# One queue order for conversions and splits, and three passes on split weights for groups of 128 rows, in an attention, MoE and MoE kernel

## The chip, the cores and the metric

One core of one Trainium2 chip. The metric is the device time of one execution in microseconds (us), the median of several runs. The engines are PE (TensorE, with its weight load PEld), DVE (VectorE), ACT (ScalarE), POOL (GpSimd) and SP (SyncE, which here issues most DMAs). Each engine takes its instructions in the order of the program and waits on semaphores.

## The reference

Three layers one after the other, in float32:

```python
# attention: 4 batches, 8 heads, 576 positions, 64 wide; window of 128, ALiBi slopes
scores = where(mask, scale * q @ k.T + bias, -1e9)
x = softmax(scores) @ v                      # as [2304, 512]
# first MoE (a dense MLP): w_in 512 x 2048, w_out 2048 x 512, float64 inputs taken as pairs of words
x = softplus(x @ w_in) @ w_out
# second MoE: 8 experts, top 2 of noisy logits; w1 512 x 1024, w2 1024 x 512 each
noisy = x @ w_gate + softplus(x @ w_noise) * noise
out[rows of expert e] += weight * (relu(x[rows] @ w1[e]) @ w2[e])
```

The result must hold to float32-like accuracy, so a product of two numbers is made of three matmuls on a high and a low half (hi·hi, hi·lo, lo·hi) in the type fp32r, or of one matmul on plain float32.

## The kernel before

The tokens go in 9 chunks of 256 (`NCH`), the hidden width of the first MoE in 16 pieces of 128 (`NF`). A job (c, f) is the up step `mm1` and, three jobs later, the down step `mm2` of piece f for chunk c. The first pieces (`NA` = 6) of chunk 0 and chunk 1 are interleaved, then those of each later chunk; attention runs beside them, a piece of it after each step (`side_work`), since chunk c needs its attention rows. The other ten pieces of all chunks follow.

The first MoE's weights come as 32 tiles of 64-bit words. `w_convert` turns one into high and low halves: a load on SP, three ACT steps (L486, L490, L500), three DVE steps of bits (L494 to L496), an add on POOL (L512), and the subtraction that gives the low half on DVE or, for some, on POOL (L504); eight are stored to DRAM and read back. At most five conversions (`NCV`) are under way; 12 may be started before the first job, the others with the jobs.

Attention's step a makes scores (PE L339), adds bias and takes the row minimum (DVE L350), exponentials (ACT L356), reciprocals (DVE L361, L362), and normalises on POOL (L370) or ACT (L368). Step b transposes (PE L201), step c multiplies with v (PE L190) and makes the high and low halves of x (ACT L429, DVE L434).

The softplus of `mm1` takes ACT, DVE and POOL steps (L565 to L574); L568, which reads the PSUM tile, frees it for PE.

The second MoE works on groups of rows of one expert: 18 pairs (256 rows) and 5 small groups (128 rows) that always run, and 2 more under a condition. The first four pairs are built from an early table, the others after the last routing. A group's w1 and w2 come as 4 tiles of 512 KB each. For pairs the order of load is one w1 tile, one w2 tile, and so on; for a small group four w1 tiles, then four w2 tiles (`WJ`). `w2_load` loads a tile as soon as the ring of 24 slots has room; `w2_split` makes its halves, `whi` on ACT (L1141) and `wlo` on DVE (L1139), for at most `NSPLIT` = 5 tiles that are not yet used up; `w2_free` runs when a tile's last matmul has been issued, and calls `pump`, which loads and splits again. Small groups use the unsplit float32 tile, and `skip_singles` passes them over when splitting.

At each step `s1` (up) of an item runs, then the transposes of the next group's rows, `s2` (transposes of a small group's hidden rows) of the item before, and `s3` (down) of the item two before. So a group's last `s3` stands after the first two `s1` of the group that follows. A pair has 8 items, a small group 2.

What sets the order on the engines is the class `Order`, a planner that runs while the program is written. `chain` gives it steps with an engine and an estimated cost; `need` and `spend` move its clock on along PE. Steps are taken from a heap by the time at which they become ready, and their instructions are issued in that order. PE's own instructions are issued directly, in the order of the loops.

Of the kernel before, what the change touches and what calls it, by code (L numbers as in the profile page):

```python
# [9 lines left out]
F32 = mybir.dt.float32  # L10
# [15 lines left out]
class Order:  # L26
# [8 lines left out]
        self.free = {}  # L35
        self.parked = {}

    def chain(self, *steps, after=0.0):

        heapq.heappush(self.heap, (self.now + after, self.count, steps, 0))  # L40
        self.count += 1

    def done(self, key, when):
# [2 lines left out]
            heapq.heappush(self.heap, (max(when, entry[0]),) + entry[1:])  # L46

    def _pop(self):
        entry = when, count, steps, i = heapq.heappop(self.heap)
        eng, cost, fn, key, needs = (tuple(steps[i]) + (None,) * 5)[:5]  # L50
        for n in needs or ():
            if n not in self.fin:
                self.parked.setdefault(n, []).append(entry)
                return
            if self.fin[n] > when:
                heapq.heappush(self.heap, (self.fin[n], count, steps, i))
                return
        if eng is not None:
            when = max(when, self.free.get(eng, 0.0))
        end = when + cost  # L60
        if eng is not None:
            self.free[eng] = end
        if fn is not None:
            fn()
        if key is not None:
            self.done(key, end)
        if i + 1 < len(steps):
            heapq.heappush(self.heap, (end + (0.1 if eng is not None else 0.0), count, steps, i + 1))

    def emitted(self, key):  # L70
        while key not in self.fin:
# [24 lines left out]
def ca(n):  # L96
    return 0.16 + n * 0.00083
# [15 lines left out]
def moe_chain_kernel(ctx, tc, qk, v, w_in, w_out, w_gate, w_noise, noise, w1, w2, out):  # L113
# [362 lines left out]
    def w_convert(i):  # L476
        fc, half = divmod(i, 2)
        d = {}

        def load():  # L480
            raw = d["raw"] = wpool.tile([P, 512, 2], I32, name="raw", tag="w", bufs=NRING)
            SP.dma_start(raw.rearrange("p n z -> p (n z)"), (w_out if half else w_in).bitcast(I32)[fc])

        def first():
            d["a"] = tl(mid, [P, 512], I32, "cva", 4, ("wl", i))
            ACT.activation(f32(d["a"]), f32(d["raw"][:, :, 1]), AF.Abs)  # L486

        def third():
            lo32 = d["raw"][:, :, 0]
            ACT.activation(lo32, lo32.bitcast(U32), AF.Copy, scale=2.0 ** -29)  # L490

        def bits():
            a = d["a"]
            DVE.tensor_scalar(f32(a), f32(a), F64_LO, F64_HI, op0=OP.max, op1=OP.min)  # L494
            DVE.tensor_scalar(a, a, 3, 0x3FFFFFFF, op0=OP.logical_shift_left, op1=OP.bitwise_and)  # L495
            DVE.scalar_tensor_tensor(a, d["raw"][:, :, 1], -0x40000000, a, op0=OP.bitwise_and, op1=OP.bitwise_or)  # L496

        def high():
            W[i] = w_tile()
            ACT.activation(W[i][:, 0], f32(d["a"]), AF.Copy)  # L500

        def low():
            t = W[i]
            (DVE if (i < 2 * NA or LOWV[i % len(LOWV)]) else POOL).tensor_tensor(t[:, 1], f32(d["a"]), f32(t[:, 0]), OP.subtract)  # L504

        def store():
            if i in sidx:
                SP.dma_start(scratch[sidx.index(i)], f32(W.pop(i)).rearrange("p z n -> p (z n)"))
                nfreed[0] += 1
        chain(("SP", 0.06, load), ("DMA", (1 << 19) / 330e3, None), (None, 2.0, None),  # L510
              ("A", ca(512), first), ("A", ca(512), third), ("V", 2.2, bits),
              ("P", cg(512), lambda: POOL.tensor_tensor(d["a"], d["a"], d["raw"][:, :, 0], OP.add), ("wa", i)),  # L512
              ("A", ca(512), high),
              ("V", cv(512), low, ("wl", i)) if (i < 2 * NA or LOWV[i % len(LOWV)]) else ("P", cg(512), low, ("wl", i)),
              (None, 0.0, lambda: mark_now(("w", i), ("wl", i))),
              ("SP", 0.06, store, ("st", i)))

    def mark_now(key, of):
        o_.done(key, o_.fin[of])
# [533 lines left out]
    def g_transpose(g, a):  # L1053
        n, eo, i = groups[g]
        d = GR[g]
        pt = ps_t(("gx", g, a)).rearrange("p (c t) -> p c t", c=KC)
        for kc in range(KC):
            tr(pt[:, kc, :], d["xg"][a][:, kc * P:(kc + 1) * P], ident)
        if n == 1:
            d["xT"] = tl(p2, [P, KC, P], F32, "xs", 2, ("gup", g))  # L1060
            return chain(("A", ca(512), lambda: ACT.activation(d["xT"], pt, AF.Copy), ("gx", g, a)))
        if a == 0:
            d["xT"] = tuple(tl(mid, [P, KC, CT], F32R, x, 2, ("gup", g)) for x in ("xh", "xl"))
        xh, xl = d["xT"]
        sl = slice(a * P, (a + 1) * P)
        chain(("A", ca(512), lambda: ACT.activation(xh[:, :, sl], pt, AF.Copy)),
              ("V", cv(512), lambda: DVE.tensor_sub(xl[:, :, sl], pt, f32(xh[:, :, sl])), ("gx", g, a)))
# [20 lines left out]
    def w2_load():  # L1088
        j = wl[0]
        if j >= NW:  # L1090
            return False
        g, kind, f = WJ[j]
        if g >= sure[0] or ("tab", 2 if groups[g][0] == 1 else int(g >= NEARLY)) not in o_.fin:
            return False
        more = len(extra) < NXTRA
        if not more and (nback[0] < len(sidx) or ring_left() < 1 + 2 * max(1, NSPLIT - nsplit[0])):
            return False
        wl[0] += 1
        n, eo, i = groups[g]
        if g not in REG:  # L1100
            REG[g] = SP.value_load(TB[eo][0:1, 0, i:i + 1], min_val=0, max_val=E - 1)
            g_rows(g)
            if g < 3 or g - 3 in turned:
                g_start(g)
        if more:
            extra.add(j)
            t = p2.tile([P, 1024], F32, name="raw2", tag="raw2", bufs=NXTRA)
        else:
            inring[0] += 1
            t = wpool.tile([P, 1024], F32, name="rawp", tag="w", bufs=NRING)  # L1110
        RAW2[j] = t
        SP.dma_start(t, (w2 if kind else w1)[bass.ds(REG[g], 1), f].rearrange("e p n -> p (e n)"))
        chain(("SP", 0.5, None), ("DMA", (1 << 19) / 280e3, None), (None, 2.5, None, ("r2" if n == 2 else "w2", j)))
        if n == 1 and wsp[0] == j:
            skip_singles()
        return True

    turned = set()
# [2 lines left out]
        n = groups[g][0]  # L1121
        chain(("P", 1.3 * n, lambda: g_gather(g), ("gg", g), (("rows", g),)), (None, 3.0, None, ("gl", g)))

    def skip_singles():
        while wsp[0] < wl[0] and groups[WJ[wsp[0]][0]][0] == 1:
            wsp[0] += 1

    def w2_split():
        skip_singles()
        j = wsp[0]  # L1130
        if j >= wl[0] or not splitting[0] or nsplit[0] >= NSPLIT or nback[0] < len(sidx) or ring_left() < 2:
            return False
        wsp[0] += 1
        nsplit[0] += 1
        t = RAW2[j]
        hi, lo = W2[j] = [wpool.tile([P, 1024], F32R, name=x, tag="w", bufs=NRING) for x in ("whi", "wlo")]

        def low():
            DVE.tensor_sub(lo, t, f32(hi))  # L1139
            w2_drop(j)  # L1140
        chain(("A", ca(1024), lambda: ACT.activation(hi, t, AF.Copy), None, (("r2", j),)),  # L1141
              ("V", cv(1024), low, ("w2", j)))
        return True

    def w2_drop(j):
# [11 lines left out]
                pass  # L1157

    def w2_free(j):
        if W2.pop(j, None) is None:  # L1160
            w2_drop(j)
        else:
            nsplit[0] -= 1
        pump()

    def parts(j, a):
        hl = W2[j]
        if WJ[j][1] == 0:
            return lambda z, kc: hl[z][:, kc * 256 + a * P:kc * 256 + (a + 1) * P]
        return lambda z: hl[z][:, a * 512:(a + 1) * 512]  # L1170
# [4 lines left out]
    def s1(g, f):  # L1175
# [15 lines left out]
        else:  # L1191
            need(("gx", g, 0))
            ph = tl(psum, [P, 512], F32, "h", 2, ("hr2", g, f))
            for x in range(2):
                j = WJ.index((g, 0, 2 * f + x))
                need(("w2", j))
                for kc in range(KC):
                    mm(ph[:, x * 256:(x + 1) * 256], GR[g]["xT"][:, kc, :],
                       RAW2[j][:, kc * 256:(kc + 1) * 256], kc == 0, kc == KC - 1)
                w2_free(j)  # L1200
            hs = tl(p2, [P, 512], F32, "hs", 2, ("ht", g, f))
            chain(("A", ca(512), lambda: ACT.activation(hs, ph, AF.Relu), ("hr2", g, f)))
# [4 lines left out]
    def s2(g, f):  # L1207
        if groups[g][0] == 2:
            return
        need(("hr2", g, f))  # L1210
        hs = H2[g, f]
        pt = ps_t(("hT", g, f)).rearrange("p (c t) -> p c t", c=4)
        for x in range(4):
            tr(pt[:, x, :], hs[:, x * P:(x + 1) * P], ident)
        mark(("ht", g, f))
        th = tl(p2, [P, 4, P], F32, "th", 2, ("dn", g, f))
        chain(("A", ca(512), lambda: ACT.activation(th, pt, AF.Copy), ("hT", g, f)))
        H2[g, f] = th

    def s3(g, f):  # L1220
# [12 lines left out]
        else:  # L1233
            need(("hT", g, f))
            th = H2.pop((g, f))
            for x in range(4):
                ff = 4 * f + x
                j = WJ.index((g, 1, ff // 2))
                need(("w2", j))
                mm(Y2[g][0], th[:, x, :], RAW2[j][:, x % 2 * 512:x % 2 * 512 + 512], ff == 0, ff == NF1 - 1)  # L1240
                if x % 2:
                    w2_free(j)
        mark(("dn", g, f))
# [208 lines left out]
```

## Time and profile before

| | us |
|---|---|
| median of 3 runs | 1137.41 (1136.45 to 1138.78) |
| the profiled execution, its own time | 1136.42 |
| its span, first to last instruction | 1134.2 |
| PE busy | 1071.8 |
| DVE busy | 748.8 |
| ACT busy | 616.2 |
| POOL busy | 509.9 |

The span is that of the one execution that was profiled; its own time also holds what lies around the span. Busy times are sums over the span and mix stages with different limits. The ends of matmuls are modelled, so a busy PE is not PE at its peak.

### The profile page before, as it was taken

How to read it: one execution, taken by the hardware profiler on the slowest of the kernel's cores; microseconds unless marked ns; L12 is line 12 of the kernel's file. 1: busy time of each engine (PE TensorE's matmuls, PEld its weight loads, DVE VectorE, ACT ScalarE, POOL GpSimd, SP SyncE). 2: the span in 40 equal slices, each digit the busy share in tenths (PEclk: the TensorE clock that was granted, in tenths of full speed). 3: DMA queues.
4: the chain of work that ended last, by engine and by line, in shares of the span. 5: the costliest groups of instructions: out<-in, count | busy, mean ns of one | idle time of the engine just before them, and what ended most of it. 6: DMA issues, size and time to landing. Idle time of an engine off the chain costs nothing.

```text
span 1134.2 us, 20933 instructions
## 1 busy us (share of the span) xinstructions
PE 1071.8 (94%) x7021; PEld 914.2 (81%) x7021; DVE 748.8 (66%) x1946; ACT 616.2 (54%) x1459; POOL 509.9 (45%) x535
## 2 busy tenths in 40 slices
PE   5589999999999999999998997999999999999997
PEld 3477777777789888888887886997997997999984
DVE  8975799988885677777767685653653653655520
ACT  7876778877764444444444543553553553555531
POOL 3455677766675566666674232222122223222112
PEclk8699999999999999999999998999999999999999
DMA  8231544554683322112348829788887888888722
GB/s 306 102 94 57 181 161 141 202 206 146 199 318 121 121 76 75 52 62 76 96 153 304 251 28 339 206 233 263 227 233 259 232 227 254 250 225 233 215 56 38
DMA packets 96557, 198.90 MB, mean 175 GB/s; under 512 B 34049, under 2 KB 44801, under 8 KB 96449
## 3 DMA queue, kind: packets, MB, share of 16 engines
q1 hardware_dynamic: 86112, 176.01, 47.2%
q0 software_dynamic: 10336, 21.54, 9.6%
q8 instruction: 56, 0.92, 0.3%
q14 instruction: 53, 0.43, 0.1%
HBM read 157.82 MB, written 39.69 MB: 174 GB/s over the span
## 4 chain that ended last, share of the span: by engine, by line
PE 76%; DVE 11%; DMA 5%; ACT 3%; issue 2%; POOL 1%; SPq 1%; POOLq 0%; DVEq 0%; ACTq 0%
PE h L190 35%; PE y L190 24%; PE z L190 10%; PE t L201 4%; PE t L190 3%; PE t L339 2%; DMA raw<-in_moe_w_out 1%; DVE s L350 1%; ACT s L356 1%; DVE w L504 1%; DVE cva L495 1%; DMA rawp<-in_moe_w 1%; DVE cva L496 1%; DVE cva L494 1%; DVE su L573 1%
## 5 line engine op out<-in xcount | busy, mean ns | idle before, releaser
L190 PE MATMUL h<-xh,w 128*128 128x256 f32 x1152 | 238.8, 290 | 4.3 <-DVE sl L568 4.2
L1139 DVE TENSOR_TENSOR wlo<-rawp,whi 128x1024 fp32r<-128x1024 f32 x107 | 130.7, 1222 | 133.8 <-ACT whi L1141 127.4
L1249 POOL DMA_INDIRECT out<-ys,rc x41 | 83.3, 2031 | 272.3 <-DVE ys L1258 131.9
L190 PEld LDWEIGHTS h<-xh,w 128*128 128x128 f32 x1152 | 190.7, 193 | 18.2 <-DVE sl L568 9.3
L1141 ACT ACTIVATE whi<-rawp 128x1024 fp32r<-128x1024 f32 x107 | 113.4, 1060 | 149.1 <-PE h L190 98.0
L190 PE MATMUL y<-w,gh 128*128 128x512 f32 x552 | 179.3, 406 | 0.1
L190 PE MATMUL h<-xh,whi 128*128 128x256 f32 x576 | 165.5, 287 | 6.5 <-DVE gl L1188 6.5
L190 PE MATMUL h<-xl,w 128*128 128x256 f32 x576 | 164.2, 285 | 3.1 <-DVE xl L434 3.1
L574 POOL TENSOR_TENSOR su<-sa,su 128x256 f32<-128x256 f32 x144 | 112.6, 782 | 113.1 <-DVE su L573 98.3
L190 PE MATMUL h<-xl,whi 128*128 128x256 f32 x576 | 163.3, 284 | 0.0
L190 PE MATMUL h<-xh,wlo 128*128 128x256 f32 x576 | 163.3, 283 | 0.0
L565 ACT ACTIVATE sa<-h 128x256 f32<-128x256 f32 x144 | 54.8, 381 | 157.5 <-PE h L190 116.0
L190 PEld LDWEIGHTS h<-xh,whi 128*128 128x128 f32 x576 | 110.1, 191 | 14.1 <-DVE gl L1188 6.9
L569 POOL TENSOR_TENSOR sl<-sl,su 128x256 f32<-128x256 f32 x144 | 109.7, 762 | 17.3 <-DVE sl L568 5.8
L190 PEld LDWEIGHTS h<-xl,w 128*128 128x128 f32 x576 | 111.1, 193 | 6.4 <-DVE xl L434 3.5
L190 PEld LDWEIGHTS h<-xl,whi 128*128 128x128 f32 x576 | 110.2, 191 | 7.1 <-issue 1.4
L190 PEld LDWEIGHTS h<-xh,wlo 128*128 128x128 f32 x576 | 110.2, 191 | 0.0
L190 PEld LDWEIGHTS y<-w,gh 128*128 128x128 f32 x552 | 95.0, 191 | 16.9 <-issue 3.2
L190 PE MATMUL y<-w,gl 128*128 128x512 f32 x276 | 108.6, 393 | 0.0
L1048 POOL DMA_INDIRECT xg<-x1buf,rc x41 | 42.4, 1035 | 105.6 <-DVE rc L1037 60.4
L572 DVE TENSOR_TENSOR gl<-sl,gh 128x256 fp32r<-128x256 f32 x144 | 81.0, 563 | 9.4 <-ACT gh L570 6.6
L370 POOL TENSOR_TENSOR s<-s,st 128x512 f32<-128x512 f32 (+2 forms) x72 | 72.2, 1011 | 33.2 <-DVE st L362 19.4
(256 smaller groups left out, 2281.5 us busy)
## 6 DMA issues: line engine op xcount, KB each, us to landing
rawp<-in_moe_w SPq DMA_DIRECT2D x140, 512.0 KB
raw<-in_moe_w SPq DMA_DIRECT2D x44, 512.0 KB
qkT<-in_qk SPq DMA_DIRECT2D x20, 512.0 KB
raw<-in_moe_w_in SPq DMA_DIRECT2D x16, 512.0 KB
raw<-in_moe_w_out SPq DMA_DIRECT2D x16, 512.0 KB
out<-zero SPq DMA_DIRECT2D x19, 256.0 KB
xspill<-xh SPq DMA_DIRECT2D x9, 512.0 KB
xspill<-xl SPq DMA_DIRECT2D x9, 512.0 KB
```

The source lines that it names most:

```text
L190: PE.matmul(o, l, r, start=start, stop=stop)
L201: PE.transpose(o, i, idn)
L339: PE.matmul(ps[j][:nq, x, :n].rearrange("p (s t) -> p s t", t=P), qkT[hd, u % NQK, 0, hp, :nq], qkT[hd, sl, 1, hp, :], start=True, stop=True)
L370: POOL.tensor_tensor(s[:nq, :, :n], s[:nq, :, :n], st[:nq, 3, 2 * x:2 * x + 2, None].to_broadcast([nq, 2, n]), OP.mult)
L565: chain(("A", ca(CT), lambda: ACT.activation(a, ph, AF.Abs)), ("A", ca(CT), lambda: ACT.activation(a, a, AF.Exp, scale=-1.0), ("e", t)), ( ...
L569: ("P", cg(CT), lambda: POOL.tensor_add(l, l, u), None, (("d", t),)),
L572: ("V", cv(CT), lambda: DVE.tensor_sub(gl, l, f32(gh)), ("g", t)))
L574: ("P", cg(CT), lambda: POOL.tensor_tensor(u, a, u, OP.subtract), ("d", t)), after=2 * ca(CT) + 0.15)
L1048: POOL.indirect_dma_start(out=x, out_offset=None, in_=x1buf[:T - 3 * CT if g < NEARLY else TPAD, :], in_offset=bass.IndirectOffsetOnAxis(a ...
L1139: DVE.tensor_sub(lo, t, f32(hi))
L1141: chain(("A", ca(1024), lambda: ACT.activation(hi, t, AF.Copy), None, (("r2", j),)), ("V", cv(1024), low, ("w2", j)))
L1249: POOL.indirect_dma_start(out=out[:, :], out_offset=bass.IndirectOffsetOnAxis(ap=rc[:, a, 0:1], axis=0), in_=ys, in_offset=None, compute_o ...
```

## The change

In `Order`, `chain` takes a rank `later`. A step whose engine is taken is put back with the time at which the engine comes free, and among steps of one time the lower rank goes first, then the older chain. The chains of `w_convert` and of `w2_split` get later=1.

Groups of 128 rows are split as pairs are: their tiles are no longer passed over, the transposed rows and the transposed hidden rows get a high and a low half (one more DVE subtraction each), and each up and down matmul on float32 becomes three on fp32r.

```diff
-    def chain(self, *steps, after=0.0):
+    def chain(self, *steps, after=0.0, later=0):
-        heapq.heappush(self.heap, (self.now + after, self.count, steps, 0))
+        heapq.heappush(self.heap, (self.now + after, later, self.count, steps, 0))
...
     def _pop(self):
-        entry = when, count, steps, i = heapq.heappop(self.heap)
+        entry = when, later, count, steps, i = heapq.heappop(self.heap)
...
-        if eng is not None:
-            when = max(when, self.free.get(eng, 0.0))
+        if eng is not None and self.free.get(eng, 0.0) > when:
+            heapq.heappush(self.heap, (self.free[eng], later, count, steps, i))
+            return
...
     def w_convert(i):
...
-              ("SP", 0.06, store, ("st", i)))
+              ("SP", 0.06, store, ("st", i)), later=1)
...
     def g_transpose(g, a):
...
-        if n == 1:
-            d["xT"] = tl(p2, [P, KC, P], F32, "xs", 2, ("gup", g))
-            return chain(("A", ca(512), lambda: ACT.activation(d["xT"], pt, AF.Copy), ("gx", g, a)))
         if a == 0:
             d["xT"] = tuple(tl(mid, [P, KC, CT], F32R, x, 2, ("gup", g)) for x in ("xh", "xl"))
...
     def w2_load():
...
-        chain(("SP", 0.5, None), ("DMA", (1 << 19) / 280e3, None), (None, 2.5, None, ("r2" if n == 2 else "w2", j)))
-        if n == 1 and wsp[0] == j:
-            skip_singles()
+        chain(("SP", 0.5, None), ("DMA", (1 << 19) / 280e3, None), (None, 2.5, None, ("r2", j)))
...
-    def skip_singles():
-        while wsp[0] < wl[0] and groups[WJ[wsp[0]][0]][0] == 1:
-            wsp[0] += 1
...
     def w2_split():
-        skip_singles()
...
-              ("V", cv(1024), low, ("w2", j)))
+              ("V", cv(1024), low, ("w2", j)), later=1)
...
     def w2_free(j):
-        if W2.pop(j, None) is None:
-            w2_drop(j)
-        else:
-            nsplit[0] -= 1
+        del W2[j]
+        nsplit[0] -= 1
         pump()
...
     def s1(g, f):
...
                 need(("w2", j))
+                w = parts(j)
+                xh, xl = GR[g]["xT"]
                 for kc in range(KC):
-                    mm(ph[:, x * 256:(x + 1) * 256], GR[g]["xT"][:, kc, :],
-                       RAW2[j][:, kc * 256:(kc + 1) * 256], kc == 0, kc == KC - 1)
+                    for n_, (l, r) in enumerate(((xh, 0), (xh, 1), (xl, 0))):
+                        mm(ph[:, x * 256:(x + 1) * 256], l[:, kc, :P], w(r, kc),
+                           kc + n_ == 0, kc == KC - 1 and n_ == 2)
                 w2_free(j)
...
     def s2(g, f):
...
-        th = tl(p2, [P, 4, P], F32, "th", 2, ("dn", g, f))
-        chain(("A", ca(512), lambda: ACT.activation(th, pt, AF.Copy), ("hT", g, f)))
+        th = [tl(p2, [P, 4, P], F32R, x, 2, ("dn", g, f)) for x in ("th", "tl")]
+        chain(("A", ca(512), lambda: ACT.activation(th[0], pt, AF.Copy)),
+              ("V", cv(512), lambda: DVE.tensor_sub(th[1], pt, f32(th[0])), ("hT", g, f)))
...
     def s3(g, f):
...
-                mm(Y2[g][0], th[:, x, :], RAW2[j][:, x % 2 * 512:x % 2 * 512 + 512], ff == 0, ff == NF1 - 1)
+                w = parts(j, x % 2)
+                for n_, (l, r) in enumerate(((0, 0), (0, 1), (1, 0))):
+                    mm(Y2[g][0], th[l][:, x, :], w(r), ff + n_ == 0, ff == NF1 - 1 and n_ == 2)
```

## Rows read from the trace of the kernel before

**Rows 1.** Busy time by stage: stage, length, five engines, granted clock, DMA share, GB/s.

```profile
15.50:71.00 55.50, 33.41 (x229) 24.74 (x230) 54.27 (x137) 45.61 (x124) 29.23 (x24) 0.75 0.35 130
71.00:115.00 44.00, 42.16 (x334) 34.08 (x331) 24.89 (x102) 29.26 (x103) 23.72 (x31) 1.00 0.27 81
...
160.00:311.00 151.00, 143.96 (x1095) 114.35 (x1095) 135.40 (x380) 114.22 (x358) 105.28 (x114) 0.98 0.53 181
...
704.00:1094.00 390.00, 390.00 (x2418) 345.24 (x2417) 208.11 (x322) 191.96 (x295) 98.53 (x62) 1.00 0.81 229
```

**Rows 2.** PE's waits, 15.5 to 71 us: in total, times, longest.

```profile
PE y L201 <- POOL s L370: 10.2, 2, 5.8
PE t L201 <- POOL s L370: 6.1, 3, 3.4
PE h L339 <- DVE st L350: 3.3, 1, 3.3
```

**Rows 3.** Groups of instructions by line, DVE, 15 to 71 us.

```profile
L504 DVE TENSOR_TENSOR w<-cva,w 128x512 fp32r<-128x512 f32 x12 | 9.4, 789 | 0.0
```

**Rows 4.** The chain that ended last, 27 to 115 us: start, length, what.

```profile
27.39 0.60 DVE w L504
27.99 1.45 DVE cva L494
...
47.46 0.35 DVE cva L494
...
47.83 0.44 DVE cva L495
...
48.29 0.69 DVE cva L496
...
114.79 1.63 PE h L190 x12
```

**Rows 5.** PE's waits, 71 to 330 us, the first and last of nine.

```profile
PE t L190 <- DVE st L350: 3.4, 2, 2.0
...
PE t L201 <- DVE xl L434: 0.4, 1, 0.4
```

**Rows 6.** PE's waits, 585 to 710 us.

```profile
PE h L190 <- DVE sl L568: 3.3, 1, 3.3
PE t L190 <- DVE mcum L757: 2.0, 1, 2.0
```

**Rows 7.** DVE's instructions in order of time, 595 to 604 us.

```profile
596.26 3.49 DVE L1139 TENSOR_TENSOR wlo<-raw,whi 128x1024 fp32r<-128x1024 f32 x3
```

**Rows 8.** Busy time by stretch, right behind the two waits of rows 6.

```profile
603.60:606.20 2.60, 2.60 (x13) 2.60 (x14) 2.53 (x10) 0.00 (x0) 1.66 (x3) 0.55 0.86 340
...
652.60:655.00 2.40, 2.37 (x15) 2.12 (x16) 2.26 (x8) 0.99 (x1) 0.00 (x0) 1.00 0.31 55
```

**Rows 9.** The chain that ended last, 766 to 793 us, around the first small group.

```profile
767.87 3.46 PE h L190 x16
...
777.48 1.39 PE y L190 x6
778.87 1.42 PE h L190 x12
...
780.73 3.44 PE z L190 x8
```

**Rows 10.** ACT's instructions in order of time, 776 to 786 us.

```profile
778.67 1.06 ACT L1141 ACTIVATE whi<-rawp 128x1024 fp32r<-128x1024 f32 x1 [0.45 <-PE y L190]
779.64 0.67 ACT L1255 ACTIVATE ys<-y,rc 128x512 f32<-128x512 f32 x1
```

**Rows 11.** DVE's instructions in order of time, 777 to 782 us.

```profile
779.77 1.23 DVE L1139 TENSOR_TENSOR wlo<-rawp,whi 128x1024 fp32r<-128x1024 f32 x1
```

**Rows 12.** ACT's instructions in order of time, 1080 to 1084 us.

```profile
1081.06 1.06 ACT L1141 ACTIVATE whi<-raw 128x1024 fp32r<-128x1024 f32 x1 [2.22 <-PE h L190]
```

**Rows 13.** SP's DMA issues in order of time, 1060 to 1090 us.

```profile
1065.42 14.81 SPq L1112 DMA_DIRECT2D rawp<-in_moe_w  x6
```

More of the change, by code (lines that the diff above doesn't have):

```diff
@@ L55, in _pop @@
             if self.fin[n] > when:
-                heapq.heappush(self.heap, (self.fin[n], count, steps, i))
+                heapq.heappush(self.heap, (self.fin[n], later, count, steps, i))
                 return
-        if eng is not None:
-            when = max(when, self.free.get(eng, 0.0))
+        if eng is not None and self.free.get(eng, 0.0) > when:
+            heapq.heappush(self.heap, (self.free[eng], later, count, steps, i))
+            return
         end = when + cost
@@ L67, in _pop @@
         if i + 1 < len(steps):
-            heapq.heappush(self.heap, (end + (0.1 if eng is not None else 0.0), count, steps, i + 1))
+            heapq.heappush(self.heap, (end + (0.1 if eng is not None else 0.0), later, count, steps, i + 1))
     def emitted(self, key):
@@ L1159, in w2_free, with parts @@
     def w2_free(j):
-        if W2.pop(j, None) is None:
-            w2_drop(j)
-        else:
-            nsplit[0] -= 1
+        del W2[j]
+        nsplit[0] -= 1
         pump()
-    def parts(j, a):
+    def parts(j, a=None):
         hl = W2[j]
+        if a is None:
+            return lambda z, kc: hl[z][:, kc * 256:(kc + 1) * 256]
         if WJ[j][1] == 0:
```

## The prediction

> **What bounds the kernel now.** Read the stages first [rows 1], then the waits of the stage in which PE stands still, then the chain of work around one group of 128 rows. In the table of stages the reader is to see two regimes. From 704 to 1094 us PE is busy 390.00 of 390 us, while DVE needs 208 and ACT 192 of them and the DMA share is 0.81: the second MoE is bound by PE alone, and what a matmul costs there is worth its full price. From 15.5 to 71 us PE is busy only 33 of 55.5 us, at a granted clock of 0.75, while DVE is busy 54.3: the start is bound by VectorE. PE's three largest waits there sum to 10.2 + 6.1 + 3.3 = 19.6 us and end on attention's normalisation (POOL L370) and score evacuation (DVE L350) [rows 2]. What holds those back is the conversion of the first MoE's weights: all 12 tiles of 2·NA are converted in this stretch [rows 3].
>
> **The order of the queues.** Before, a step takes its engine in the order in which it becomes ready. After, a step whose engine is taken waits until it is free, and then the first by (later, age) goes; conversions (load, three ACT steps, bits, add, subtraction, store, on SP, ACT, DVE and POOL alike) and splits carry later=1. The instructions, and the order on PE, stay.
>
> *The start.* A conversion costs DVE 0.35 + 0.44 + 0.69 us for its bits and 0.60 for its low half, 2.1 us [rows 4]. The job list wants only weights 0 to 4 by the fourth job; 5 to 11 are wanted one after the other until the twelfth job, whose up step starts at 114.8 us [rows 4]. So 7 of 12 can leave the stretch: 7 × 2.1 = 14.6 us less DVE work ahead of attention. They must be done from 71 to 115, where DVE is free for 44 − 24.9 = 19.1 us and ACT for 14.7 [rows 1]; they nearly fill it, so I give a quarter back and take 11 us. Bounds: nothing, if PE then waits for weights, and 19.6 us, if every wait of [rows 2] goes.
>
> *A rule against it.* DVE's L494 takes 0.35 us in one place and 1.45 in another [rows 4]. The Trainium skill (SBUF — State Buffer, "Who interferes with whom") has VectorE and GpSimd share a port pair that one instruction holds to its end. By that page the moved conversions meet GpSimd's softplus additions from 71 to 115 us and are drawn out there as well; taking 1.1 us more for each of the seven, as an estimate, 8 us would be given back and the time would be some 4 us above my forecast.
>
> *Attention beside the first MoE, 71 to 330 us.* PE's waits are nine rows of 3.4 down to 0.4 us, 10.8 in all [rows 5], mostly for attention's DVE steps. DVE is busy 135 of 151 us from 160 to 311, so most remain: I take 3 us, between 0 and 8.
>
> *The entry of the second MoE.* The first five splits, three of them 3.49 us [rows 7], stand ahead of a softplus step on DVE, and PE waits 3.3 us for that step [rows 6]; then 2.6 us of matmuls run at a clock of 0.55 [rows 8], which loses 1.2. Ranked last, the splits stand behind it; PE still has the last jobs of the first MoE to run before it wants their first tile. I take all 4.5 us; bounds 0 and 4.5. What is late next is the rows of the fifth group, which the order leaves as they are.
>
> Order together: 11 + 3 + 4.5 = 18.5 us.
>
> **Three passes for the groups of 128 rows.** Five such groups run. *Removed:* 2 × 3.46 us up and 2 × 3.44 us down, 13.8 us a group [rows 9]. *Added:* up, 24 passes of 256 columns for each f, in the form whose 12 take 1.42 us, so 2 × 2.84; down, 12 passes of 512 columns, whose 6 take 1.39, so 2 × 2.78; 11.24 us. Saved 2.56 us a group, 12.8 us in all, all on PE's path.
>
> *The splits.* 40 tiles more: 40 × 1.06 us on ACT and 40 × 1.23 on DVE [rows 10, 11], and three DVE subtractions of 512 columns a group, each half a split's width. DVE would stand at some 270 and ACT at 235 of 390 us: hidden on average, by PE's work.
>
> *The wait that this adds.* At most NSPLIT = 5 tiles may be split and not yet used. Before, groups of 128 were skipped, so the five were the next pair's. After, tiles are split in load order, and a small group loads its four w1 tiles and then its four w2 tiles. Follow the steps: when its second up step ends, its four w1 tiles are free and the four w2 tiles split; the fifth place is held by the pair's last w2 tile, which is freed by the y matmuls at 777.48. The very next PE instructions, h at 778.87 [rows 9], want the *next* group's first tile, whose split may be issued only at that release. The trace shows that a split starts at the release: whi at 778.67 with y's end [rows 10]. Now the group's evacuation ys (0.67) goes ahead of it on ACT, then whi 1.06, then wlo 1.23: 2.96 us, of which a little overlaps; I take 2.9. PE takes its instructions in order, so all behind h waits too: the group's transposes, its down passes, and through them ys and the store. This happens at four transitions (three to a pair, one from the fourth small group to the fifth): 11.6 us. In that last one the fifth group's second w1 tile is capped in the same way by its first: 2.3 us (whi and wlo) once more, or nothing if it can start early because no loads compete; the nearest row, a split after the last loads were issued [rows 13], still starts at PE's release [rows 12], so I take 2.3. Together 13.9 us; bounds 0 (the split is in fact ready) and 14.7 (3.1 each, if another split is in the way).
>
> *The clock.* A wait of 3.3 us was followed by 2.6 us at 0.55; one of 2.0 us was followed by a clock of 1.00 [rows 6, 8]. 2.9 is nearer to the first: 4 × 1.2 = 4.8 us; bounds 0 and 6 (five times).
>
> Together: 12.8 − 13.9 − 4.8 = −5.9 us, a loss, between −7.9 and +12.8.
>
> **Sum.** 18.5 − 5.9 = 12.6 us less. The profiled execution took 1136.42 us (span 1134.2); 1123.8. The median of before, 1137.41, is 1.0 above it, so 1125 for the median.
>
> **Rivals.**
> *The splits are ready in time.* If the split of the next group's first tile is hidden, the three passes keep their 12.8 us: 1137.4 − 18.5 − 12.8 = 1106. For it: ACT and DVE have room. Against: the count of five.
> *Late weights take the place of late attention; slower.* If the conversions, ranked last on engines that are nearly full, reach PE as waits on L190's weights before 115 us, or if they slip into the gaps of 0.1 us that the plan leaves between steps and so are not moved at all, the start and the attention stage give nothing. Then 5.9 us are lost and at most 4.5 won at the entry: 1139 to 1143. It decides where the order wins less than 5.9 us. For it: DVE is busy 54.3 of 55.5 us whatever the order [rows 1]. Against: 19.1 us of room right behind, and weights 5 to 11 are not wanted sooner.
> *DMA bounds the small groups.* Eight tiles of 512 KB in 11.2 us are 374 GB/s; the stage moves 229 at a share of 0.81, so some 283 at most, 14.8 us a group. Then the three passes give nothing, neither gain nor more loss: 1137.4 − 18.5 = 1119. Against: the last six loads are all issued by 1080 us [rows 13], while PE is fully busy until 1094 and beyond [rows 1] with tiles that came before them.
>
> **How the numbers follow.** Forecast 0.52, splits ready 0.17, late weights 0.23, DMA 0.08. The forecast's own range is 1113 to 1134: its order terms each from a third to their upper bound, its loss from 2 to 7.9. To leave out no more than 2 in 10 the range reaches down to the first rival and up into the second: 1105 to 1141. A change of this kernel under 0.2% (2.3 us) can't be told from none. Faster: 0.49 of the forecast, 0.17, 0.08 and 0.02 of late weights, 0.76. Same: 0.02 and 0.06, 0.08. Slower: 0.01 and 0.15, 0.16.
>
> **What the changed profile would show.** PE's full load (before: from 71 us [rows 1]) begins near 60; PE's waits from 15.5 us until then are at most 12 us, and conversions stand on DVE after it. No wait of 3 us on L568 at the entry. Up steps of the small groups of about 2.85 us in place of 3.46, down steps of 2.78. After each of the first four, a PE wait of 2.3 to 3.1 us before h, released by wlo, and a lower clock behind it. The prediction is wrong if those waits are missing (then about 1106 to 1112), if PE waits for the first MoE's weights before 115 us, or if the loads of the second MoE land late.

## The result and the profile after

The changed kernel takes 1151.03 us (median of four, 1149.14 to 1154.66) against 1136.93 for the kernel before beside it: a ratio of 1.0126, 95% interval 1.0103 to 1.0148. It is slower by 14 us, where 12.6 us less were forecast, and lies outside the range of 1105 to 1141. The profiled execution has a span of 1149.7 us, 15.5 more than before.

Where the 15.5 us went is read from events that both traces have: the issue on SP of each chunk's `xspill<-xh` (its attention rows are ready), the last chunk's `x1buf<-x` (the first MoE is done), and the end. These are the changed kernel's, in order of time (start, length, what):

```profile
32.78 0.33 SPq L553 DMA_DIRECT2D xspill<-xh  x1
59.45 0.33 SPq L553 DMA_DIRECT2D xspill<-xh  x1
113.43 0.33 SPq L553 DMA_DIRECT2D xspill<-xh  x1
...
635.08 0.38 SPq L645 DMA_DIRECT2D x1buf<-x  x1
```

| event | before | after | order alone (e1) | with readiness (e4) |
|---|---|---|---|---|
| chunk 0's spill | 43.09 | 32.78 | 31.95 | 32.87 |
| chunk 1's spill | 71.98 | 59.45 | 57.58 | 58.71 |
| chunk 2's spill | 115.14 | 113.43 | 112.92 | 115.89 |
| chunk 8's spill | 307.31 | 317.61 | 318.52 | 307.40 |
| last `x1buf` | 622.28 | 635.08 | 635.93 | 621.28 |
| end of the span | 1134.2 | 1149.7 | 1143.2 | 1130.1 |

The two columns on the right belong to experiments below. The second column against the first: 12.5 us are won by chunk 1's spill, 10.8 of them are gone by chunk 2's; from there to chunk 8's another 12.0 are lost (204.2 us in place of 192.2), 2.5 by the last `x1buf`, and 2.7 from there to the end.

A line number of the kernel before is two higher in the changed kernel up to the second MoE (L504 is L506), and three higher in e4. The stages, which answer to [rows 1] (after the length, busy time of PE, PEld, DVE, ACT and POOL with counts, then the granted clock, DMA share and GB/s):

```profile
15.50:71.00 55.50, 43.82 (x320) 32.57 (x320) 48.30 (x144) 49.42 (x146) 29.15 (x28) 0.85 0.50 165
71.00:115.00 44.00, 36.65 (x258) 29.20 (x255) 33.08 (x98) 26.43 (x85) 25.37 (x28) 0.92 0.13 43
160.00:311.00 151.00, 135.91 (x1026) 107.47 (x1024) 132.19 (x372) 110.45 (x344) 100.92 (x110) 0.97 0.48 165
704.00:1094.00 390.00, 379.94 (x2440) 344.55 (x2440) 246.16 (x364) 212.51 (x317) 98.24 (x63) 0.99 0.81 237
```

PE gained 10 busy us up to 71 and lost 5.5 in the next row, 8 in the third and 10 in the last. DVE's load did move: 54.27 to 48.30 us in the first row, 24.89 to 33.08 in the second.

**Late weights, 60 to 115 us.** PE's waits (in total, times, longest):

```profile
PE h L192 <- DVE w L506: 5.3, 2, 4.3
PE t L203 <- DVE st L352: 2.5, 2, 1.3
PE t L341 <- DVE sdl L436: 0.5, 1, 0.5
```

The first did not exist before; in this stretch the kernel before waits 5.3 us in all, and for no weight. The chain that ended last shows what stood ahead of the weight of the longest wait (start, length, what):

```profile
73.66 0.60 DVE w L506
74.27 0.33 DVE pT L401
74.60 0.56 DVE cva L496
75.19 0.44 DVE cva L497
75.65 0.69 DVE cva L498
76.34 0.34 DVE gl L574
76.67 1.19 DVE st L363
...
80.58 1.11 DVE w L506
81.73 2.50 PE h L192 x10
```

From its last step of bits, at 75.65, to 80.58 this tile goes through POOL and ACT and then waits on DVE behind softplus and attention steps. Ten matmuls right after the wait take 2.50 us, at a granted clock of 0.50; twelve take 1.42 elsewhere [rows 9].

From chunk 1's spill to chunk 2's, PE runs as many matmuls in both kernels (the first row is the kernel before, columns as above):

```profile
71.98:115.14 43.16, 41.33 (x324) 33.41 (x323) 24.68 (x101) 28.45 (x99) 23.66 (x30) 1.00 0.27 83
59.45:113.43 53.98, 45.66 (x324) 36.28 (x324) 43.23 (x121) 35.42 (x112) 32.99 (x37) 0.93 0.26 76
```

So of the 10.8 us lost here, 6.5 are PE standing still (8.3 us in place of 1.8, of which 5.3 for weights), and 4.3 are the same matmuls taking longer at a clock of 0.93.

**Attention, 115 to 330 us.** The largest of PE's waits, to read against [rows 5]:

```profile
PE t L192 <- ACT pT L399: 8.7, 5, 4.4
PE t L203 <- DVE st L352: 2.0, 2, 1.0
PE t L203 <- POOL s L372: 2.0, 1, 2.0
```

From 115 to 318 us all waits sum to 18.6 us, before to 8.6. `pT`, the evacuation of attention's transposed rows, stood at 0.7. ACT's instructions in order of time around the longest wait show why:

```profile
170.94 0.66 ACT L488 ACTIVATE cva<-raw 128x512 f32<-128x512 f32 x1 [4.44 <-DMA raw<-in_moe_w_in]
171.51 0.49 ACT L358 ACTIVATE s<-s,st 128x256 f32<-128x256 f32 x1
...
173.78 0.36 ACT L567 ACTIVATE sa<-h 128x256 f32<-128x256 f32 x1
174.04 0.36 ACT L399 ACTIVATE pT<-t 128x256 f32<-128x256 f32 x1
```

ACT stands 4.44 us behind a conversion whose tile has not landed; the kernel before has such a stall too, 3.55 us, up to 168.45. But before, `pT` follows the stalled conversion by 0.84 us; here four exponentials, with their reads of the accumulator, and two softplus steps go first, and it follows by 3.10. The exponentials' chain is the older, since their scores stand ahead of the transposes in PE's order; `pT` is what PE's next matmul reads.

**The small groups, 788 to 794 us, around the first.** ACT and DVE in order of time, then the two stretches from 788.9 (columns as above):

```profile
788.28 0.70 ACT L1253 ACTIVATE ys<-y,rc 128x512 f32<-128x512 f32 x1
788.85 1.07 ACT L1133 ACTIVATE whi<-rawp 128x1024 fp32r<-128x1024 f32 x1
```
```profile
788.21 0.74 DVE L1256 TENSOR_SCALAR ys<-y,rc 128x512 f32<-128x512 f32 x1
788.87 2.35 DVE L1131 TENSOR_TENSOR wlo<-rawp,whi 128x1024 fp32r<-128x1024 f32 x2
```
```profile
788.90:791.30 2.40, 0.53 (x3) 0.33 (x3) 2.32 (x3) 1.02 (x2) 2.07 (x1) 0.94 0.78 213
791.30:793.90 2.60, 2.60 (x12) 2.60 (x13) 0.00 (x0) 0.09 (x1) 0.28 (x1) 0.50 0.99 183
```

The split of the next group's first tile starts when the pair's last y matmul has run, behind the evacuation `ys`. PE waits 1.86 us for `whi`, does two matmuls that need no `wlo`, waits 0.79 for `wlo`, and goes on at a clock of 0.50. Over all small groups, 720 to 1150 us, PE's waits are these two rows, where the kernel before has none:

```profile
PE h L192 <- ACT whi L1133: 7.4, 4, 1.9
PE h L192 <- DVE wlo L1131: 3.3, 4, 0.9
```

### The profile page after: what moved, and what is told of

It reads as the page before. It is cut to its first block, busy times and chain, and to the rows that moved or that the text cites. A ratio compares the mean times of both kernels' runs of the same rounds, so it can differ in the third digit from the quotient of the medians.

```text
span 1149.7 us, 21198 instructions
## 1 busy us (share of the span) xinstructions
PE 1071.9 (93%) x7141; PEld 925.9 (81%) x7141; DVE 812.7 (71%) x2001; ACT 653.3 (57%) x1499; POOL 511.1 (44%) x535
## 4 chain that ended last, share of the span: by engine, by line
PE 70%; DVE 15%; ACT 5%; DMA 3%; issue 2%; POOL 2%; SPq 0%; POOLq 0%; DVEq 0%; ACTq 0%
PE h L192 33%; PE y L192 21%; PE z L192 9%; PE t L203 3%; PE t L192 2%; DVE su L575 2%; ACT s L358 2%; DVE wlo L1131 2%; DVE s L352 2%; DVE gl L574 1%; PE t L341 1%; DVE cva L497 1%; DVE sl L570 1%; DVE cva L498 1%; DVE cva L496 1%
## 5 line engine op out<-in xcount | busy, mean ns | idle before, releaser
L1247 POOL DMA_INDIRECT out<-ys,rc x41 | 81.0, 1976 | 283.2 <-DVE ys L1256 126.0
L1131 DVE TENSOR_TENSOR wlo<-rawp,whi 128x1024 fp32r<-128x1024 f32 x140 | 169.0, 1225 | 32.2 <-ACT whi L1133 24.3
L1179 ACT ACTIVATE gh<-h 128x256 fp32r<-128x256 f32 x144 | 55.3, 384 | 213.6 <-PE h L192 207.8
L576 POOL TENSOR_TENSOR su<-sa,su 128x256 f32<-128x256 f32 x144 | 109.7, 761 | 98.0 <-DVE su L575 76.3
L1133 ACT ACTIVATE whi<-rawp 128x1024 fp32r<-128x1024 f32 x140 | 145.7, 1056 | 12.0 <-PE z L192 6.1
L1180 DVE SCALAR_TENSOR_TENSOR gl<-h,gh 128x256 fp32r<-128x256 f32 x144 | 60.5, 420 | 115.8 <-ACT gh L1179 110.9
L571 POOL TENSOR_TENSOR sl<-sl,su 128x256 f32<-128x256 f32 x144 | 112.8, 783 | 24.8 <-DVE rec L706 5.6
```

Source lines behind the costliest of these rows:

```text
L571: ("P", cg(CT), lambda: POOL.tensor_add(l, l, u), None, (("d", t),)),
L576: ("P", cg(CT), lambda: POOL.tensor_tensor(u, a, u, OP.subtract), ("d", t)), after=2 * ca(CT) + 0.15)
L1179: chain(("A", ca(CT), lambda: ACT.activation(gh, ph, AF.Relu)), ("V", cv(CT), lambda: DVE.scalar_tensor_tensor(gl, ph, 0.0, f32(gh), op0=O ...
L1180: ("V", cv(CT), lambda: DVE.scalar_tensor_tensor(gl, ph, 0.0, f32(gh), op0=OP.max, op1=OP.subtract), ("hr2", g, f)))
L1247: POOL.indirect_dma_start(out=out[:, :], out_offset=bass.IndirectOffsetOnAxis(ap=rc[:, a, 0:1], axis=0), in_=ys, in_offset=None, compute_o ...
```

## The experiments

| run | median, us | ratio, 95% interval |
|---|---|---|
| e1 order alone | 1145.35 | 1.0073, 1.0055 to 1.0090 |
| e2 three passes alone | 1141.95 | 1.0048, 1.0031 to 1.0064 |
| e3 put-back and age, no ranks | 1165.60 | 1.0266, 1.0233 to 1.0299 |
| e4 order, readiness for age | 1133.72 | 0.9970, 0.9958 to 0.9981 |
| e5 as e4, conversions not ranked | 1136.60 | 0.9987, 0.9972 to 1.0002 |
| e6 as e2, cap 6 | 1127.99 | 0.9902, 0.9883 to 0.9921 |
| e7 all, readiness, cap 6 | 1130.26 | 0.9938, 0.9920 to 0.9955 |
| e8 all, readiness, cap 5 | 1141.53 | 1.0021, 1.0001 to 1.0040 |
| e9 as e2, cap 7 | 1124.41 | 0.9887, 0.9870 to 0.9903 |
| e10 as e7, splits not ranked | 1125.29 | 0.9890, 0.9874 to 0.9907 |
| e11 as e4, fewer DVE steps | 1158.59 | other weights, see there |
| e12 the change, cap 6 | 1140.10 | 1.0023, 1.0008 to 1.0037 |
| e14 as e10, cap 7 | 1123.36 | 0.9864, 0.9843 to 0.9886 |
| e16 as e4, three buffers | 1140.91 | 1.0020, 1.0003 to 1.0038 |

### The two halves alone: e1 and e2

e1 is the kernel before with the hunks of `Order` and the two `later=1`; e2 is the changed kernel with these taken back.

```diff
 e1, on the kernel before
-        if eng is not None:
-            when = max(when, self.free.get(eng, 0.0))
+        if eng is not None and self.free.get(eng, 0.0) > when:
+            heapq.heappush(self.heap, (self.free[eng], later, count, steps, i))
+            return
 e2, on the changed kernel: the same lines the other way round
```

> Only the queue order of the change (put back until the engine is free, then rank, then age; conversions and splits last); groups of 128 rows as before. If the three passes cost what the changed profile shows (three transitions of 2.1 us, the end even: 6.4 us), this kernel is some 6 us faster than the changed one, about 1144, and still 7 us slower than before. If the order is harmless and the loss comes from splits that crowd DVE and ACT, it is at or below 1137.

> Only the three passes on split weights; the queue order as before. Theory of the cap of five splits: a wait of 2.3 to 3.1 us before the first up step of each group that follows a small one, net 5 to 7 us slower than before, about 1143. Rival (splits ready in time): 12 us faster, about 1124.

The order costs 0.73% and the passes 0.48%; their sum is 1.21%, the change 1.26%. So they act side by side, and the order, forecast to gain 18.5 us, is the larger loss. Its events stand in the table above: the attention stage is as late as with both parts, and from the last `x1buf` to the end it takes 507.3 us where the kernel before takes 511.9.

### Which part of the order: e3 and e4

e3 keeps the put-back and the tie-break by age and gives no rank. e4 keeps put-back and ranks, and breaks a tie of rank by the time at which the step became ready, then by age.

```diff
 e3, on the changed kernel without its passes
-              ("SP", 0.06, store, ("st", i)), later=1)
+              ("SP", 0.06, store, ("st", i)))
...
 e4
-            heapq.heappush(self.heap, (self.free[eng], later, count, steps, i))
+            heapq.heappush(self.heap, (self.free[eng], later, ready, count, steps, i))
```

> Only the put-back with age as the tie-break; no chain has a rank. Theory A (age order harms: the youngest chains, attention's transposed scores and high halves, which PE wants next, wait for every older chain): slower than before by 8 us or more, 1145 or above, with PE's waits between 113 and 318 us as in the changed kernel or longer. Theory B (it is the rank that harms, since late conversions come in bunches): within 3 us of before.

> As e1_order, but among steps of one rank the one that became ready first goes first, not the oldest chain. Theory A: the harm between 113 and 318 us goes, the start's gain of some 10 us stays at least in part: 1125 to 1135. Theory B: as e1_order, about 1144.

e3 is the slowest of all. Its chunk 0 spills at 65.83 us (before 43.09), for the conversions, started first, are now the oldest chains and go ahead of attention everywhere. PE's wait in the view of 15.5 to 60 us:

```profile
PE y L203 <- POOL s L372: 34.0, 2, 17.5
```

e4's waits from 115 to 330 us begin with these rows:

```profile
PE t L193 <- DVE st L353: 4.3, 4, 2.1
PE t L204 <- POOL s L373: 2.2, 3, 1.1
PE h L193 <- DVE sl L571: 1.5, 1, 1.5
```

`pT` is gone from them; from 115 to 318 us they sum to 9.8, and chunk 8 spills at 307.40, as before the change. From chunk 2's spill to chunk 8's the kernel before takes 192.2 us, e1 205.6 and e3 204.9, both by age, e4 191.5. So it is the age, not the put-back or the ranks, that lost the 12 us of attention. e4 gains 0.3%, about 3.4 us; its trace has 3.1 of the 4.1 us of its span after the last `x1buf`. Up to 115 us nothing stays of the start.

### What gives the start back: e5, e11 and e16

```diff
 e5, on e4: conversions not ranked, splits last
-              ("SP", 0.06, store, ("st", i)), later=1)
+              ("SP", 0.06, store, ("st", i)))
...
 e11, on e4: two of the three bit steps left out of the first 12 conversions
+            if i >= 2 * NA:
                 DVE.tensor_scalar(f32(a), f32(a), F64_LO, F64_HI, op0=OP.max, op1=OP.min)
                 DVE.tensor_scalar(a, a, 3, 0x3FFFFFFF, op0=OP.logical_shift_left, op1=OP.bitwise_and)
...
 e16, on e4: three running values in place of four
-            d["a"] = tl(mid, [P, 512], I32, "cva", 4, ("wl", i))
+            d["a"] = tl(mid, [P, 512], I32, "cva", 3, ("wl", i))
```

> As e4_ready (tie-break by readiness), but only splits are ranked last; conversions have the rank of all others. Theory (the start's gain of 13 us at the second chunk's spill is spent on late weights before 115 us, so ranking conversions is worth nothing in the end): the spills of the first chunks fall back to about 43 and 72 us, the third stays near 115, and the time is that of e4_ready within 3 us, 1131 to 1137. Rival (the rank of conversions carries e4_ready's 4 us): 1137 or above.

> As e4_ready, but the first 12 conversions leave out the DVE steps that clamp and shift (L494, L495 of the kernel before), so the weights are wrong. If DVE's capacity bounds the way to the third chunk (PE waits for weights there because DVE has the same work to do, only later), the third spill comes earlier by most of the 15.6 us that these 24 steps took in e4_ready: at 101 to 107 us in place of 115.9. If it is the length of a conversion's chain of steps at the lowest rank, it comes earlier by no more than 4 us.

> The order with readiness and ranks, small groups unsplit as before, and three buffers in place of four for a conversion's running value, so that three conversions instead of four can be between their first and last step. Theory 'length of a conversion's chain times those under way': a conversion spends most of its time waiting for engines at the lowest rank, so three of four under way convert about a quarter slower; PE's waits for the first MoE's weights, 8.6 us in all between 60 and 115 us with four, grow by 8 us or more and the third chunk's spill comes after 121 us instead of 115.9. Rival 'VectorE has no room': the work and the engines are the same; the waits stay at 6 to 11 us and the spill at 114 to 118.

e5 spills at 42.86, 72.08 and 115.18 us, which is the kernel before; its 115.18 and e4's 115.89 are the same place reached with and without the ranked conversions. Up to there the rank brings attention forward and the weights back, one for one. The interval of e5's ratio holds 1, and e4's overlaps it.

e11's weights send tokens to other experts and a sixth small group ran, so only its times up to 300 us can be read. With DVE 7.5 us less busy from 15.5 to 98 us (64.86 for 72.41), chunk 2's spill moves from 115.89 to 113.64 and PE still waits 5.8 us for weights, after 8.6. That speaks against DVE's room as the whole cause, with one limit: the planner still books 2.2 us of DVE for the shortened step, so the room was freed on the chip and not in the plan that sets the order. The edit also makes the chain of steps shorter.

e16 went the way of its first theory in one number, the spill of chunk 2 at 123.86, and not in the other: its waits for weights from 60 to 115 us did not grow.

```profile
PE h L193 <- DVE w L507: 4.5, 1, 4.5
PE t L204 <- POOL s L373: 3.8, 1, 3.8
PE t L204 <- DVE st L353: 3.6, 2, 2.3
PE h L193 <- ACT w L503: 1.4, 1, 1.4
```

The delay is there by chunk 1's spill (68.98, e4 58.71) and in attention's waits. By its code, with fewer buffers the planner must also finish older conversions before it goes on, which puts them ahead of attention; no run shows this by itself. So the pace of conversion depends on how many may be under way, but the run does not tell their waiting at the lowest rank apart from this side effect. More buffers were not tried, and this stays open.

### The cap and the place of the splits: e6 to e10, e12 and e14

```diff
 e6 on e2, e12 on the change, e7 on the change with readiness (cap 7 in e9 and e14)
-    NSPLIT = 5
+    NSPLIT = 6
...
 e10, on e7, and e14: splits not ranked, conversions still last
-              ("V", cv(1024), low, ("w2", j)), later=1)
+              ("V", cv(1024), low, ("w2", j)))
```

e8 is the change with readiness in place of age, and the cap left at 5.

> As e2_passes (old queue order, three passes), but six tiles may be split and unused in place of five. Theory of the cap: the next group's first tile is split while PE is still in the small group, the waits of some 3 us at three transitions go, and the passes keep 2.5 us a group: 10 to 17 us faster than e2_passes, 1125 to 1132. Rival (ACT and DVE can't keep up, or two more slots of the ring make loads late): within 3 us of e2_passes, 1139 to 1145.

> The changed kernel with tie-break by readiness and six splits. If both repairs add: e4_ready's 1134 less the 12.6 us of the passes, 1118 to 1124.

> The changed kernel with tie-break by readiness in place of age and nothing else. If age costs what e1_order and e4_ready differ by (11.6 us) here too: 1151 - 12 = 1139; the passes' 4 to 6 us of loss are left, so it is slower than e4_ready by that.

> As e6_cap6 with seven splits. With six, PE's waits behind the small groups are 1.0 us for wlo in all and the last pair of small groups still asks for a tile whose place is freed only just before. If those are all that is left, seven gains 0 to 4 us, 1124 to 1128; if the two slots less of the ring make the loads late, it is slower than e6_cap6.

> As e7_both6, but splits keep the rank of all others; only conversions are last. In e7_both6 PE still waits 6 us behind the small groups for splits that stand last. If the rank of the splits makes these waits, they fall to 1 or 2 us, and the time to 1122 to 1128; if not, 1130.

> The changed kernel with six splits and nothing else (age as the tie-break stays). If cap and age add as separate causes: 1151 less the 11 to 14 us that six splits gained in e6_cap6 and e7_both6, 1137 to 1140, as fast as before; the attention stage stays 10 us late.

> The change with readiness in place of age, conversions still ranked last, splits not ranked, and a cap of seven. If the cap and the unranked splits are all that the small groups lack, and readiness all that attention lacks, this equals the version with the old planner and a cap of seven (ratio 0.989) within 0.3%: 1121 to 1127 us; the waits for whi and wlo behind the small groups stay under 1 us in all. If ranking the conversions has a gain of its own beyond the old order, it is 1121 or less.

One more place turns the three passes from a loss of 0.48% (e2) into a gain of 0.98% (e6). e2's waits for `wlo` and `whi` were 5.9 and 4.2 us; e6 keeps one of 1.0. A seventh removes that too (e9), and the gain is 1.13%, 12.9 us. It is near the 12.8 worked out for the passes, but it is not theirs alone. Where the splits were late, e6 and e9 wait 3.9 and 3.7 us in all for `xl`, the low half of the next group's transposed rows. And a wait far from the small groups is gone. In the kernel before it is PE's longest from 585 to 725 us, and [rows 6] leaves it out:

```profile
PE h L190 <- DVE gl L1188: 6.5, 1, 6.5
```

It ends at 698.75 us; DVE stands idle for 9.23 us ahead of it, until a DMA has brought `rk`, the records of a group's rows. e2 (6.0), e4 (6.8), e5 and e8 (6.4) and e7 (5.4) have it too, the changed kernel, e1 and e12 2.0 to 3.0 of it. It is absent in e6, e9, e10 and e14, which have a larger cap and splits that are not ranked. The larger cap was not run on the kernel before, so how the gain parts between the passes and this wait is not shown.

e7 missed its 1118 to 1124: with the sixth place its splits still wait, because they stand last. PE's waits from 725 us on:

```profile
PE h L193 <- DVE wlo L1132: 4.8, 4, 1.3
PE h L193 <- ACT whi L1134: 1.3, 4, 0.3
```

e12 has the same two sums. Without the rank of the splits (e10) they shrink to one of 1.0, and the ratio goes from 0.9938 to 0.9890; the wait of 5.4 us on `gl` goes with them, and 3.9 us for `xl` come. e8, with the cap of 5, has 7.4 and 3.1, close to the change; the order's tie-break does nothing for them. e12 ends at 1.0023, with chunk 8's spill at 316.89: the cap is worth some 1.0% and the age stays.

e14 puts the mended parts together and is the fastest run, 1.36% under the kernel before. PE waits from 585 us on:

```profile
PE h L193 <- DVE xl L1067: 3.9, 4, 1.3
PE h L193 <- DVE sl L571: 3.7, 2, 2.2
PE t L193 <- DVE mcum L760: 3.0, 1, 3.0
PE t L193 <- DVE r_mb L707: 0.8, 1, 0.8
```

No wait on a split is left; of the first row 3.7 us stand at three small groups, as in e9. But its interval overlaps e9's, which has the old planner; whether the order adds to the three passes and the larger cap is not shown.

## Why the prediction was wrong

The forecast gave the order −18.5 us and the passes +5.9. By its own steps:

*The start* (11 us won): the sizing of the gain was right, 10.3 us at chunk 0's spill and 12.5 at chunk 1's, with PE's waits from 15.5 to 60 us at 10.7 in all. At chunk 1's spill five of the twelve tiles still lack their bits and six their low halves, at the prices of [rows 4] 11.0 us of DVE work moved behind. The step that failed is that the conversions fit in from 71 to 115 us at the price of a quarter. All but 1.7 us were gone at 115. It is the rival of late weights, in the form that the prediction named: PE waits on weights before 115. The prediction set a stage's free time against its work (19.1 us on DVE) and took the work to be hidden. DVE still had 44.00 − 33.08 = 10.9 us free there; a weight is late by its own eight instructions over three engines, each of which can stand behind others. That this is the cause rather than DVE's room is supported in part by e11 and not settled by e16, and stays open. The waits are only part of it: 6.5 of the 10.8 us are PE standing still, the other 4.3 its lower clock, for which the prediction had no term here.

*The rule against it.* The Trainium skill (SBUF — State Buffer, "Who interferes with whom") was taken to draw the moved conversions out, at an estimate of 8 us. From 71 to 115 us the five `w` subtractions average 832 ns, where the twelve before average 789 [rows 3], and the three steps each of L496 and L497 770 and 667 ns, where before they average 727 and 630: about 0.04 us each, 0.5 us in all. Counted from chunk 1's spill on, at 59.45, five steps each of L496, L497 and L498 average 688, 773 and 895 ns (before 727, 630 and 693) and six subtractions 814: 1.7 us more in all. In e4 the twelve subtractions average 957 ns up to 120 us, some 2 us in all, and the bits together no more than before. Single ones are drawn out in both places alike (up to 1.6 us before the change). So the traces bear out at most 2 of the 8 us. Five low halves came after 71 us, not seven.

*Attention from 71 to 330 us* (3 us won, bounds 0 to 8). This is the step with the wrong sign and the largest miss. The prediction quoted the rule, "the first by (later, age)", and never asked who is oldest. The conversions were ranked last, but attention's chains were not equal among themselves: the youngest are those that PE waits for next. From 115 us on it cost 12.0 us to chunk 8's spill. e4 shows the cause by changing the tie-break alone. No rival had attention losing, so late weights at 1139 to 1143 missed the time as well.

*The entry of the second MoE* (4.5 us won): the wait was right, the gain was not. The wait on L568, 3.3 us up to 603.60 before, is absent there in the changed kernel and 0.2 in e4 and e5. It stands ahead of the last `x1buf`; from chunk 8's spill to that event order alone takes 2.4 us more than the kernel before, e5 0.4 more and e4 1.1 less. The forecast named the fifth group's rows as late next; what came is the routing's `r_mb`, 0.6 us before and 3.2 after (2.6 in e4), and in order alone and the changed kernel two waits for `x` of 2.7. From the last `x1buf` to the end order alone takes 4.6 us less, e4 3.1, e5 3.9. That this is near 4.5 does not bear the term out: in order alone the wait on `gl` near 700 us, which the prediction did not have, is 2.1 us in place of 6.5. e4 and e5 keep that wait and lose the one for `mcum` [rows 6]; the rest of their gain is not traced.

*The three passes* (5.9 us lost): mechanism and place were right, the size in part by luck. In the first small group, from its first h to the end of its second z, the kernel before takes 21.15 us and the changed one 23.29: 2.1 us lost, forecast 2.9 + 1.2 − 2.56 = 1.5. The four waits are 10.7 us in all for the 4 × 2.9 forecast, and the cap of 5 is their cause (e6, e9). The clock fell behind three of the four, at some 4.3 us for the 4.8 forecast (last section). The fifth term, 2.3 us in the last group, was wrong: between that group's first and second up step stand the y passes of the group before, 1126.91 to 1129.77 us, and PE stands still for 0.05 us only. Without it the sum is 12.8 − 11.6 − 4.8 = −3.6. e2 loses 0.48%, 5.5 us, but in its trace only 2.9 of 4.4 us are lost after the last `x1buf`; 1.5 are there at chunk 8's spill (308.81), where no small group runs.

*Splits ready* (1106) fell at a cap of 5. *DMA bound* fell too: from 725 us on no wait of PE ends on a load of weights, and in e9 and e14, at the same DMA share of 0.81, only the waits for `xl` are left.

## What to carry to other kernels

A planner's tie-break is a change of order for every chain, not only for those that get a rank: before costing it, write down which chain is oldest at each tie and which one the bound engine wants next. Work that is moved behind is not hidden because an engine's free time adds up; ask when its last step lands, over all its engines, and who reads it. And when a cap counts things in use, follow one transition step by step: here one place more turned a loss of 0.5% into a gain of 1%, if not at that place alone.

## What the hardware showed that was not expected

Waits of one length were not followed by one clock. Each of the four waits behind the small groups of the changed kernel is split in two by two matmuls, 2.65 to 2.72 us in all. In the 2.6 us right behind the first and the fourth (from 791.27 and 1122.31 us) the granted clock is 0.50, the 1.2 GHz level. Behind the second and the third (columns as above):

```profile
878.78:881.38 2.60, 2.60 (x15) 2.60 (x16) 0.42 (x1) 0.39 (x1) 0.31 (x1) 0.69 0.70 205
966.43:969.03 2.60, 2.60 (x18) 2.47 (x19) 0.46 (x2) 0.98 (x2) 0.33 (x1) 1.00 0.74 194
```

The second fell later, and the 2.6 us after that row are at 0.66. As an estimate from these clocks, time at a clock c loses the share 1 − c: 1.3, 1.7, 0 and 1.3 us, 4.3 in all. In the kernel before a wait of 2.0 us was followed by a clock of 1.00 and one of 3.3 by 0.55 [rows 6, 8], but in e14 one of 3.0 us, up to 656.00, by 1.00. So the prediction's way of pricing the clock, by the length of the wait alone, came near in the sum and does not hold for each wait.
